# Attention scores in float32r: two heads on separate rows of the array instead of one wide product over both heads

## The chip, the cores and the metric

One core of a Trainium2 chip runs the whole program. The metric is the device time of one execution in microseconds (us); the kernel before takes 942.9 us, the median of three runs (940.86 to 945.25).

## The reference, cut to what matters

A linear-attention layer (batch B = 4, H = 8 heads, S = 768 positions, D = 48 channels per head) feeds two mixture-style layers of matrix products:

```python
for t in range(S):
    cur = np.einsum('bhd,bhe->bhde', u[None] * kt, vt)
    y[:, :, t] = np.einsum('bhd,bhde->bhe', rt, state + cur)
    state = w[None, :, :, None] * state + np.einsum('bhd,bhe->bhde', kt, vt)
...
x = y as [B*S, H*D]                       # 3072 x 384
m = ((x @ w_a) * (x @ w_b)) @ w_out       # d_ff 1536
out = (((m @ w1) * (m @ w2)) @ w3) @ w_out2   # d_ff 1024
```

All data are float32.

## The kernel before

**Tiling.** The positions are cut into 6 chunks of C = 128. A *unit* u is one chunk of one batch element: u = 4c + b, 24 units in all; "step c" is the four units of chunk c. The 8 heads lie in 4 pairs p; a pair has its first head in partitions 0 to 47 and its second in 64 to 111 (`XR`, line 179), 112 partitions in all. Inside a chunk the recurrence is written with matrices: per head a 128x128 matrix of scores k-times-r (functions `scores`, `scores_f`), masked and given its diagonal (`a_evac`, `a_diag`), then y = state times r plus scores times v (`y_mm`, lines 408 to 421), and the state is moved on by k times v (`s_mm`, `s_decay`, `s_upd`).

**Two ways to compute the scores.** Units 0 to 3 are done ahead (`scores_0`). Units 4 to 7 (u < `U_R` = 8) take `scores_f`, line 364: plain float32, for each pair p one 48x128 by 48x128 product per head, the two heads on rows 0 to 47 and rows 64 to 111 of the array, each head into its own PSUM tile (one tile for the first heads of all pairs, one for the second heads). From unit 8 on (step 2) the kernel splits k and r into a float32r high part and a float32r rest (`kth`, `ktl`; `rbh`, `rbl`) and adds three products, high-high, high-rest, rest-high (lines 381 to 383). There r lies in a tile of 256 columns per pair: columns 0 to 127 hold the first head in partitions 0 to 47, columns 128 to 255 the second head in partitions 64 to 111, and everything else is zero (memsets, lines 594 and 595). So one product over 112 rows with 128 columns of weights and 256 moving columns gives both heads; a PSUM tile holds two pairs, and `scores` is called in two halves, `scores(u, 0)` and `scores(u, 1)`.

**The order of heads.** Which half holds which head follows from this: with `scores_f` the halves of the score tile are "all first heads, all second heads" (0, 2, 4, 6, 1, 3, 5, 7), with the wide product they are 0, 1, 2, ... 7. `head(u, i)` on line 358 says so, and `y_mm` goes through the heads in that order: its product for head h writes rows 0 to 47 of the output for an even h and 64 to 111 for an odd one, that is, it uses one or the other half of the array's columns (48 columns of weights).

**What sets the order of the work.** The schedule is written by hand. `unit_slots` (line 508) cuts a unit into 8 slots; slots of the units of chunk q+1 are merged (`merge`, line 539) between the pieces of the first mixture layer on chunk q: `ab_mm` (line 631, products of 128x128 weights and 512 columns in float32r) and `m_mm` (line 676). Slot 0 has `scores(u, 0)` and the scaling of the next unit's r, slot 1 `scores(u, 1)` and `a_evac` of the first half, slot 2 the second half and `prep_hi` (the casts to float32r on ScalarE), slots 3 and 4 `prep_rl` (the rest of r, once per head of a pair, on GpSimd), slot 4 `y_mm` and `s_mm`, slot 5 the evacuation of y and `prep_kl`, slot 6 `s_upd`, which adds the new part to the state on VectorE. Scores, y and the state's products all take their PSUM tile from one pool of two buffers (`ps_at`, line 176, tile name `at`), in turn.

Of the kernel before, what the change touches and what calls it, by code (L numbers as in the profile page):

```python
# [7 lines left out]
F32 = mybir.dt.float32  # L8
F32R = mybir.dt.float32r
# [4 lines left out]
ALU = mybir.AluOpType  # L14
# [5 lines left out]
NP = H // 2  # L20
C = 128
# [30 lines left out]
U_R = 2 * B  # L52
# [102 lines left out]
def rwkv_moe_kernel(ctx, tc, rkT, nat, wu, wab, wout, w12, w3T, wo2, r_in, k_in, v_in, w_in, u_in, out):  # L155
    nc = tc.nc
    mm = nc.tensor.matmul
# [5 lines left out]
    def flat(ap):  # L163
        return ap.rearrange("p a b -> p (a b)")

    with tc.manual_schedule():
        const = tc.alloc_tile_pool(name="const", bufs=1, side="left")
        wabp = tc.alloc_tile_pool(name="wabp", bufs=1, side="left")
        att = tc.alloc_tile_pool(name="att", bufs=2, side="left")
# [6 lines left out]
        ps_at = tc.alloc_tile_pool(name="ps_at", bufs=2, space=PSUM)  # L176
        k_0 = xtp.tile([128, 2, B, DM], F32, tag="xt", name="k_0")[:, 0]

        XR = [(0, D), (64, 64 + D)]
# [5 lines left out]
        def load_rk(u):  # L185
            if u < NU:
                rk_t[u] = (wabp.tile([112, 2, NP * C], F32, tag=("w1h", "w1l", "w2h", "w2l")[u], name="rk")
                           if u < B else att.tile([112, 2, NP * C], F32, name="rk"))
                nc.sync.dma_start(out=rk_t[u], in_=rkT[u])
# [3 lines left out]
        def load_nat(u):  # L193
            if u < B:
                nc.sync.dma_start(out=v_0[:, u, :], in_=nat[u, :, 2, :])
            elif u < NU:
                nat_t[u] = att.tile([128, 3, DM], F32, name="natt")
                nc.sync.dma_start(out=nat_t[u], in_=nat[u])

        def v_of(u):  # L200
            return v_0[:, u, :] if u < B else nat_t[u][:, 2, :]
# [97 lines left out]
        for p in range(NP):  # L299
            nc.vector.tensor_tensor_scan(  # L300
                out=pos[:, p, 1:], data0=wc[:, p:p + 1].to_broadcast([112, HALF]), data1=zer,
# [5 lines left out]
        nc.vector.tensor_copy(out=tk, in_=tr[:, :, ::-1])  # L307
        wC = const.tile([112, NP, 1], F32, name="wC")
        nc.vector.tensor_tensor(out=wC, in0=pos[:, :, HALF:], in1=pos[:, :, HALF:], op=ALU.mult)
        rbh = att.tile([112, NP, 2 * C], F32R, name="rbh", bufs=1)  # L310
        rbl = att.tile([112, NP, 2 * C], F32R, name="rbl", bufs=1)
        s_t = [att.tile([112, NP, 112], F32, name=f"s{b}", bufs=1) for b in range(B)]

        rf_t, kth_t, ktl_t, d_t, a_t, kn_t, at_ps, xt = {}, {}, {}, {}, {}, {}, {}, {}

        kf_t, pr_t, y3_t = {}, {}, {}

# [7 lines left out]
            eng.tensor_tensor(out=kf_t[u], in0=kf_t[u], in1=flat(tk), op=ALU.mult)  # L325

        def prep_hi(u):
            for x, (a, e) in enumerate(XR):
                nc.scalar.copy(out=rbh[a:e, :, x * C:(x + 1) * C], in_=rf_t[u][a:e])  # L329
            kth_t[u] = att.tile([112, NP * C], F32R, name="kth", bufs=1)  # L330
            nc.scalar.copy(out=kth_t[u], in_=kf_t[u])

        def prep_rl(u, x, eng):
            a, e = XR[x]
            h, l = (t[a:e, :, x * C:(x + 1) * C] for t in (rbh, rbl))
            eng.tensor_tensor(out=l, in0=rf_t[u][a:e], in1=h, op=ALU.subtract)  # L336

        def prep_kl(u, eng):
            ktl_t[u] = att.tile([112, NP * C], F32R, name="ktl", bufs=1)
# [12 lines left out]
        def k_nat(u):  # L352
            if u < NU - B:
                k = k_0[:, u, :] if u < B else nat_t[u][:, 1, :]
                kn_t[u] = k if u < B else att.tile([128, DM], F32, name="kn", bufs=1)
                nc.gpsimd.tensor_tensor(out=kn_t[u], in0=k, in1=tnat.rearrange("p a x d -> p (a x d)"), op=ALU.mult)

        def head(u, i):

            return i if u >= U_R else i % 4 * 2 + i // 4  # L360

        def scores_f(ps, r, k):

            for p in range(NP):
                s = slice(p * C, (p + 1) * C)
                for x, (r0, r1) in enumerate(XR):
                    mm(ps[x][:, p, :], lhsT=k[r0:r1, s], rhs=r[r0:r1, s], start=True, stop=True)

        def scores(u, hf):
            if u < U_R:  # L370
                if hf == 0:
                    for x in range(2):
                        at_ps[u, x] = ps_at.tile([128, NP, C], F32, name="at")
                    scores_f([at_ps[u, x] for x in range(2)], flat(rf_t[u]), kf_t.pop(u))
                return
            ps = at_ps[u, hf] = ps_at.tile([128, 4, C], F32, name="at")
            for q in range(2):
                p = 2 * hf + q
                o = flat(ps[:, 2 * q:2 * q + 2, :])
                ks = slice(p * C, (p + 1) * C)  # L380
                mm(o, lhsT=kth_t[u][:, ks], rhs=rbh[:, p, :], start=True, stop=False)
                mm(o, lhsT=kth_t[u][:, ks], rhs=rbl[:, p, :], start=False, stop=False)
                mm(o, lhsT=ktl_t[u][:, ks], rhs=rbh[:, p, :], start=False, stop=True)

        def a_evac(u, hf):
            if hf == 0:
                a_t[u] = (wop.tile([128, H, C], F32, tag=("woh1", "wol1")[u % 2], name="a_0")
                          if u < B else att.tile([128, H, C], F32, name="a_sc", bufs=1))
            nc.vector.tensor_tensor(
                out=a_t[u][:, 4 * hf:4 * hf + 4, :], in0=at_ps.pop((u, hf)),  # L390
                in1=mask.rearrange("p (o n) -> p o n", o=1).to_broadcast([128, 4, C]), op=ALU.mult)

        def a_diag(u, hf):
            d = d_t[u][:, 4 * hf:4 * hf + 4] if u >= U_R else d_t[u].rearrange("p (q x) -> p x q", x=2)[:, hf, :]
            nc.vector.copy_predicated(  # L395
                out=a_t[u][:, 4 * hf:4 * hf + 4, :],
                mask=ident.bitcast(I32).rearrange("p (o n) -> p o n", o=1).to_broadcast([128, 4, C]),
                data=d.rearrange("p (h o) -> p h o", o=1).to_broadcast([128, 4, C]))
# [9 lines left out]
        def y_mm(u):  # L408
            c, b = divmod(u, B)
            ps = at_ps["y", u] = ps_at.tile([112, NP, C], F32, name="at")  # L410
            v, a = nat_t[u][:, 2, :], a_t.pop(u)

            for p in range(NP):
                mm(ps[:, p, :], lhsT=s_t[b][:, p, :], rhs=rf_t[u][:, p, :], start=(p == 0), stop=False,  # L414
                   skip_group_check=True)
            for i in range(H):
                h = head(u, i)
                r0, r1 = XR[h % 2]
                mm(ps[r0:r1, h // 2, :], lhsT=v[:, h * D:(h + 1) * D], rhs=a[:, i, :], start=False, stop=True,  # L419
                   skip_group_check=True)  # L420
            rf_t.pop(u)
# [45 lines left out]
        def s_mm(u):  # L467
            c, b = divmod(u, B)
            v = v_of(u)
            nat_t.pop(u, None)  # L470
            if c == NC - 1:
                return
            ps = (ps_at.tile([112, NP, D], F32, name="at") if c else
                  ps_m.tile([112, NP, D], F32, tag=("m2", "m0")[u % 2], name="s_ps"))
            at_ps["s", u] = ps
            kn = kn_t.pop(u)
            for p in range(NP):
                for x, (r0, r1) in enumerate(XR):
                    hs = slice((2 * p + x) * D, (2 * p + x + 1) * D)
                    mm(ps[r0:r1, p, :], lhsT=kn[:, hs], rhs=v[:, hs],  # L480
                       start=True, stop=True)

        def s_decay(u):
            c, b = divmod(u, B)
            if c < NC - 1:
                nc.gpsimd.tensor_tensor(out=s_t[b], in0=s_t[b], in1=wC.to_broadcast([112, NP, 112]), op=ALU.mult)
# [21 lines left out]
        def unit_slots(u):  # L508
            n = u + 1
            nxt = n < NU  # L510
            pool = nc.gpsimd

            def after(f, *a):
                if nxt:
                    f(n, *a)

            def after_r(f, *a):
                if nxt and n >= U_R:
                    f(n, *a)

            return [
                lambda: (scores(u, 0), after(prep_r, pool)),
                lambda: (scores(u, 1), a_evac(u, 0), after(prep_k, pool)),
                lambda: (a_evac(u, 1), a_diag(u, 0), after_r(prep_hi), k_nat(u)),
                lambda: (a_diag(u, 1), after_r(prep_rl, 0, pool)),

                lambda: (y_mm(u), s_mm(u), after_r(prep_rl, 1, pool)),
                lambda: (load_rk(u + 2), load_nat(u + 2), y_evac(u), (u + 1) % B == 0 and y_shuffle(u // B), s_decay(u),
                         after_r(prep_kl, pool), after(prep_d, 0)),
                lambda: (s_upd(u), after(prep_d, 1)),  # L530
                lambda: after(prep_d, 2),
            ]
# [58 lines left out]
        prep_0(1)  # L591
        both_a(0)
        diag_0(0)
        nc.gpsimd.memset(rbh.bitcast(F32), 0.0)
        nc.gpsimd.memset(rbl.bitcast(F32), 0.0)
        for t in s_t:
            nc.gpsimd.memset(t, 0.0)

# [516 lines left out]
```

## Time and profile before

| | |
|---|---|
| runs | 942.9 us median (940.86, 942.9, 945.25) |
| the profiled execution | 940.6 us, its span 938.9 us |
| TensorE matmul busy | 898.6 us (96%) |
| VectorE, ScalarE, GpSimd busy | 478.8, 344.0, 306.5 us |
| mean granted TensorE clock | 0.979 of full speed |

The span is what the trace covers, from the first to the last instruction; 1.7 us of the execution lie around it. Busy TensorE time is made of records that overlap: a 512-column product is recorded with 0.39 us although the next one starts 0.23 us later. What a stretch costs is read from the starts, not from the lengths. A float32 product leaves two records, a float32r product one. The scores in float32r run from 158.9 us (unit 8) to 490.9 us (unit 23).

### The profile page before, as it was taken

The numbers are of one execution on the slowest core, as the hardware profiler recorded it, in microseconds if no ns is written. First come the engines' busy times: TensorE is split into PE (matmuls) and PEld (weight loads), VectorE is DVE, ScalarE is ACT, GpSimd is POOL, SyncE is SP. The second block draws the span as 40 slices with busy tenths as digits, with TensorE's granted clock in tenths as the row PEclk, the third lists the DMA queues.
The fourth block names the chain that finished last, engine by engine and source line by source line (L and its number), as shares of the span: only waits on it lengthen the run. The fifth ranks groups of instructions, "written<-read, shape, count | busy, mean of one in ns | idle before, by whom it ended". The sixth has DMA issues, their size and how long they took to land.

```text
span 938.9 us, 12503 instructions
## 1 busy us (share of the span) xinstructions
PE 898.6 (96%) x4898; PEld 766.0 (82%) x4898; DVE 478.8 (51%) x684; ACT 344.0 (37%) x721; POOL 306.5 (33%) x245
## 2 busy tenths in 40 slices
PE   7778889999999999999999989899999999999997
PEld 7656678888888888888888867799988888888886
DVE  8799994545344544454442777765322222323222
ACT  4555653322322232223221775755422222222221
POOL 4566766555355626543420342322200000000000
PEclk9789889999999999999999999999999999999999
DMA  9534532212212211122102435443110010100001
GB/s 276 170 115 149 165 112 62 79 46 79 61 60 75 64 59 65 46 62 80 45 1 84 146 124 159 140 157 106 34 45 23 35 35 34 34 34 1 34 1 37
DMA packets 26065, 73.56 MB, mean 78 GB/s; under 512 B 3152, under 2 KB 7376, under 8 KB 26000
## 3 DMA queue, kind: packets, MB, share of 16 engines
q1 hardware_dynamic: 26000, 72.70, 24.6%
q8 instruction: 40, 0.66, 0.3%
q14 instruction: 25, 0.20, 0.1%
HBM read 61.28 MB, written 9.44 MB: 75 GB/s over the span
## 4 chain that ended last, share of the span: by engine, by line
PE 80%; DVE 11%; DMA 4%; issue 3%; ACT 1%; SPq 0%; DVEq 0%
PE ab L635 45%; PE m L686 4%; PE m L687 4%; PE m L688 4%; PE at L783 4%; DVE cvt L114 3%; PE o L807 3%; PE o L806 3%; PE o L808 3%; DVE cvt L117 2%; PE at L419 2%; PE at L414 2%; DVE cvt L98 1%; DMA stg_t<-in_wout_dram 1%; DVE gl L666 1%
## 5 line engine op out<-in xcount | busy, mean ns | idle before, releaser
L660 DVE TENSOR_TENSOR g<-g,ab 128x512 f32<-128x512 f32 x120 | 82.2, 685 | 269.1 <-PE ab L635 261.3
L635 PE MATMUL ab<-xt,w12h 128*128 128x512 f32 x576 | 177.5, 389 | 0.0
L661 ACT CAST gh<-g 128x512 fp32r<-128x512 f32 x120 | 74.5, 621 | 263.4 <-DVE g L660 263.4
L654 ACT COPY g<-ab 128x512 f32<-128x512 f32 x120 | 70.1, 584 | 247.4 <-PE ab L635 246.9
L666 DVE TENSOR_TENSOR gl<-g,gh 128x512 fp32r<-128x512 f32 x120 | 107.1, 893 | 65.0 <-ACT gh L661 65.0
L635 PEld LDWEIGHTS ab<-xt,w12h 128*128 128x128 f32 x576 | 107.5, 188 | 18.9
L635 PE MATMUL ab<-xt,w12l 128*128 128x512 f32 x288 | 112.0, 389 | 0.0
L687 PE MATMUL m<-gl,woh 128*128 128x512 f32 x216 | 86.4, 400 | 9.0 <-DVE gl L666 9.0
L686 PE MATMUL m<-gh,woh 128*128 128x512 f32 x216 | 87.3, 404 | 1.3 <-ACT gh L661 1.3
L336 POOL TENSOR_TENSOR rbl<-rk,rbh 48x512 fp32r<-48x512 f32 x32 | 49.3, 1542 | 120.1 <-ACT rbh L329 118.9
L688 PE MATMUL m<-gh,wol 128*128 128x512 f32 x216 | 85.2, 395 | 0.0
L635 PEld LDWEIGHTS ab<-xt,w12l 128*128 128x128 f32 x288 | 54.0, 188 | 11.2
L114 DVE SCALAR_TENSOR_TENSOR cvt<-stg_t,cvt 128x512 int32<-128x512 int32 x61 | 59.2, 970 | 0.3
L687 PEld LDWEIGHTS m<-gl,woh 128*128 128x128 f32 x216 | 41.3, 191 | 19.5 <-DVE gl L666 11.6
L117 DVE SCALAR_TENSOR_TENSOR cvt<-stg_t,cvt 128x512 int32<-128x512 int32 x61 | 54.5, 893 | 0.3
L686 PEld LDWEIGHTS m<-gh,woh 128*128 128x128 f32 x216 | 41.2, 191 | 12.4 <-ACT gh L661 3.3
L635 PE MATMUL ab<-xt,wab1h 128*128 128x512 f32 x144 | 47.0, 409 | 2.5 <-ACT wab1h L136 2.5
L688 PEld LDWEIGHTS m<-gh,wol 128*128 128x128 f32 x216 | 41.3, 191 | 8.7
L395 DVE COPY_PREDICATED a_sc<-ident,dg 128x512 f32<-128x512 int32 x40 | 46.3, 1197 | 0.0
L635 PE MATMUL ab<-xt,wab0h 128*128 128x512 f32 x144 | 45.3, 396 | 0.8 <-ACT g L654 0.8
L635 PE MATMUL ab<-xt,wab3h 128*128 128x512 f32 x144 | 45.9, 400 | 0.0
L635 PE MATMUL ab<-xt,wab2h 128*128 128x512 f32 x144 | 45.8, 400 | 0.0
(283 smaller groups left out, 1805.8 us busy)
## 6 DMA issues: line engine op xcount, KB each, us to landing
natt<-in_nat_dram SPq DMA_DIRECT2D x20, 576.0 KB, 5.0
rk<-in_rkT_dram SPq DMA_DIRECT2D x24, 448.0 KB, 4.2
stg_t<-in_wab_dram SPq DMA_DIRECT2D x18, 512.0 KB, 3.6
stg_t<-in_w3T_dram SPq DMA_DIRECT2D x16, 512.0 KB, 3.6
stg_t<-in_w_dram SPq DMA_DIRECT2D x12, 512.0 KB, 3.7
stg_t<-in_wout_dram SPq DMA_DIRECT2D x9, 512.0 KB, 3.5
m_d<-m_sb SPq DMA_DIRECT2D x18, 256.0 KB, 2.3
stg_t<-m_d SPq DMA_DIRECT2D x18, 256.0 KB, 2.6
```

The lines of the kernel that those rows point to most:

```text
L114: nc.vector.scalar_tensor_tensor(out=f, in0=w[:, :, 1], scalar=-0x40000000, in1=f, op0=ALU.bitwise_and, op1=ALU.bitwise_or)
L117: nc.vector.scalar_tensor_tensor(out=f, in0=w[:, :, 0], scalar=29, in1=f, op0=ALU.logical_shift_right, op1=ALU.bitwise_or)
L336: eng.tensor_tensor(out=l, in0=rf_t[u][a:e], in1=h, op=ALU.subtract)
L395: nc.vector.copy_predicated(out=a_t[u][:, 4 * hf:4 * hf + 4, :], mask=ident.bitcast(I32).rearrange("p (o n) -> p o n", o=1).to_broadcast([ ...
L635: mm(ps, lhsT=w[i][:, k, cs], rhs=x[:, j, k, :], start=(n == 0), stop=(n == 3 * KD - 1))
L654: nc.scalar.copy(out=t["g"], in_=t["a"])
L660: nc.vector.tensor_tensor(out=g, in0=g, in1=t["b"], op=ALU.mult)
L661: nc.scalar.copy(out=gh, in_=g)
L666: nc.vector.tensor_tensor(out=gl, in0=t["g"], in1=gh, op=ALU.subtract)
L686: mm(m_ps[q][k], lhsT=wh[:, j, cs], rhs=gh, start=(f == 0), stop=False)
L687: mm(m_ps[q][k], lhsT=wh[:, j, cs], rhs=gl, start=False, stop=False)
L688: mm(m_ps[q][k], lhsT=wl[:, j, cs], rhs=gh, start=False, stop=(f == NF1 - 1))
```

## The change

Units from 8 on now use the layout of `scores_f` for the three float32r products as well: the high part and the rest of r are plain 112 x 512 tiles (`rh`, `rl`), each product takes 48 rows, 128 columns of weights and 128 moving columns, and the two heads of a pair follow each other on rows 0 to 47 and rows 64 to 111, each into its own PSUM tile. All 24 products of a unit stand in slot 0, which takes both `at` buffers at once. `head` now gives the order 0, 2, 4, 6, 1, 3, 5, 7 for every unit, `a_diag` follows it, the cast of r is one instruction, the rest of r is one instruction (slot 3), and the two memsets are gone.

```diff
-        rbh = att.tile([112, NP, 2 * C], F32R, name="rbh", bufs=1)
-        rbl = att.tile([112, NP, 2 * C], F32R, name="rbl", bufs=1)
...
         def prep_hi(u):
-            for x, (a, e) in enumerate(XR):
-                nc.scalar.copy(out=rbh[a:e, :, x * C:(x + 1) * C], in_=rf_t[u][a:e])
+            rh_t[u] = att.tile([112, NP * C], F32R, name="rh", bufs=1)
+            nc.scalar.copy(out=rh_t[u], in_=flat(rf_t[u]))
...
-        def prep_rl(u, x, eng):
-            a, e = XR[x]
-            h, l = (t[a:e, :, x * C:(x + 1) * C] for t in (rbh, rbl))
-            eng.tensor_tensor(out=l, in0=rf_t[u][a:e], in1=h, op=ALU.subtract)
+        def prep_rl(u, eng):
+            rl_t[u] = att.tile([112, NP * C], F32R, name="rl", bufs=1)
+            eng.tensor_tensor(out=rl_t[u], in0=flat(rf_t[u]), in1=rh_t[u], op=ALU.subtract)
...
         def head(u, i):
-            return i if u >= U_R else i % 4 * 2 + i // 4
+            return i % 4 * 2 + i // 4
...
-        def scores(u, hf):
+        def scores(u):
+            ps = [ps_at.tile([128, NP, C], F32, name="at") for _ in XR]
+            for x in range(2):
+                at_ps[u, x] = ps[x]
             if u < U_R:
-                if hf == 0:
...
+                scores_f(ps, flat(rf_t[u]), kf_t.pop(u))
                 return
-            ps = at_ps[u, hf] = ps_at.tile([128, 4, C], F32, name="at")
-            for q in range(2):
-                p = 2 * hf + q
-                o = flat(ps[:, 2 * q:2 * q + 2, :])
-                ks = slice(p * C, (p + 1) * C)
-                mm(o, lhsT=kth_t[u][:, ks], rhs=rbh[:, p, :], start=True, stop=False)
-                mm(o, lhsT=kth_t[u][:, ks], rhs=rbl[:, p, :], start=False, stop=False)
-                mm(o, lhsT=ktl_t[u][:, ks], rhs=rbh[:, p, :], start=False, stop=True)
+            kh, kl, rh, rl = (t.pop(u) for t in (kth_t, ktl_t, rh_t, rl_t))
+            for p in range(NP):
+                s = slice(p * C, (p + 1) * C)
+                for n, (k, r) in enumerate(((kh, rh), (kh, rl), (kl, rh))):
+                    for x, (r0, r1) in enumerate(XR):
+                        mm(ps[x][:, p, :], lhsT=k[r0:r1, s], rhs=r[r0:r1, s], start=(n == 0), stop=(n == 2))
...
-                lambda: (scores(u, 0), after(prep_r, pool)),
-                lambda: (scores(u, 1), a_evac(u, 0), after(prep_k, pool)),
+                lambda: (scores(u), after(prep_r, pool)),
+                lambda: (a_evac(u, 0), after(prep_k, pool)),
                 lambda: (a_evac(u, 1), a_diag(u, 0), after_r(prep_hi), k_nat(u)),
-                lambda: (a_diag(u, 1), after_r(prep_rl, 0, pool)),
+                lambda: (a_diag(u, 1), after_r(prep_rl, pool)),
...
-        nc.gpsimd.memset(rbh.bitcast(F32), 0.0)
-        nc.gpsimd.memset(rbl.bitcast(F32), 0.0)
```

**TensorE at unit 8, the first unit with float32r scores.** `at` is the PSUM tile of the scores, `kth` and `ktl` are the weights, `rbh` and `rbl` (now `rh`, `rl`) what moves; `ab` is the first mixture layer. Before, the first half of the unit, three wide products for each of two pairs, then six products of `ab`:

```order
L635 MATMUL ab<-xt,wab0l 128x512
L381 MATMUL at<-rbh,kth 128x256
L382 MATMUL at<-rbl,kth 128x256
L383 MATMUL at<-rbh,ktl 128x256
L381 MATMUL at<-rbh,kth 128x256
L382 MATMUL at<-rbl,kth 128x256
L383 MATMUL at<-rbh,ktl 128x256
L635 MATMUL ab<-xt,wab0h 128x512 x2
L635 MATMUL ab<-xt,wab0l 128x512
```

With the change, at the same place, the whole unit, two heads in each row (x2):

```order
L378 MATMUL at<-rh,kth 128x128 x2
L378 MATMUL at<-rl,kth 128x128 x2
L378 MATMUL at<-rh,ktl 128x128 x2
L378 MATMUL at<-rh,kth 128x128 x2
L378 MATMUL at<-rl,kth 128x128 x2
L378 MATMUL at<-rh,ktl 128x128 x2
L378 MATMUL at<-rh,kth 128x128 x2
L378 MATMUL at<-rl,kth 128x128 x2
L378 MATMUL at<-rh,ktl 128x128 x2
L378 MATMUL at<-rh,kth 128x128 x2
L378 MATMUL at<-rl,kth 128x128 x2
L378 MATMUL at<-rh,ktl 128x128 x2
```

The second half has moved up by one slot, and 12 products of 256 columns have become 24 of 128. `y_mm` keeps its place and its count; only the heads inside it change places, which the names in this list do not tell.

**GpSimd in the slots of unit 7, where unit 8 is prepared.** `s_186` and `s_184` are the same tile, the state. Before:

```order
L137 TENSOR_TENSOR wab5l<-cvt,wab5h 128x512
L336 TENSOR_TENSOR rbl<-rk,rbh 48x4x128 x2
L486 TENSOR_TENSOR s_186<-s_186,wC 112x448
L340 TENSOR_TENSOR ktl<-rk,kth 112x512
L345 TENSOR_TENSOR pr<-natt,u_bc 128x384
```

With the change:

```order
L137 TENSOR_TENSOR wab5l<-cvt,wab5h 128x512
L333 TENSOR_TENSOR rl<-rk,rh 112x512
L481 TENSOR_TENSOR s_184<-s_184,wC 112x448
L337 TENSOR_TENSOR ktl<-rk,kth 112x512
L342 TENSOR_TENSOR pr<-natt,u_bc 128x384
```

Two instructions over 48 partitions have become one over 112; nothing else moves on this engine there.

## Rows read from the trace of the kernel before

**Rows 1.** The page's first part: busy time of each engine and its share of the span.

```profile
PE 898.6 (96%) x4898; PEld 766.0 (82%) x4898; DVE 478.8 (51%) x684; ACT 344.0 (37%) x721; POOL 306.5 (33%) x245
```

**Rows 2.** Busy time of each engine in the stretch of the float32r scores; the columns are the stretch, its length, then PE, PEld, DVE, ACT, POOL, the granted clock, the share of DMA and GB/s.

```profile
158.00:497.00 339.00, 339.00 (x1973) 284.84 (x1972) 162.15 (x223) 97.67 (x178) 158.54 (x126) 1.00 0.19 57
```

**Rows 3.** TensorE in order of time, the first half of unit 15's scores with the products around it: start, length to the end of the last of its records, instruction, count.

```profile
309.17 0.39 PE L635 MATMUL ab<-xt,wab4l 128*128 128x512 f32 x1
309.39 0.28 PE L381 MATMUL at<-rbh,kth 112*128 112x256 f32 x1
309.51 0.28 PE L382 MATMUL at<-rbl,kth 112*128 112x256 f32 x1
...
310.08 0.64 PE L635 MATMUL ab<-xt,wab4h 128*128 128x512 f32 x2
310.56 0.40 PE L635 MATMUL ab<-xt,wab4l 128*128 128x512 f32 x1
```

**Rows 4.** TensorE in order of time around unit 7's float32 scores, two heads on separate rows (16 records for 8 products).

```profile
131.78 0.40 PE L635 MATMUL ab<-xt,wab4l 128*128 128x512 f32 x1
132.11 1.16 PE L367 MATMUL at<-rk 48*128 48x128 f32 x16
133.20 0.50 PE L686 MATMUL m<-gh,woh 128*128 128x512 f32 x1
133.53 0.39 PE L687 MATMUL m<-gl,woh 128*128 128x512 f32 x1
133.76 0.39 PE L688 MATMUL m<-gh,wol 128*128 128x512 f32 x1
```

**Rows 5.** The weight loads (PEld) of the same place in order of time; those of L686 and L687 are of float32r weights.

```profile
132.10 0.97 PEld L367 LDWEIGHTS at<-rk 48*128 48x128 f32 x16 [0.36 <-issue]
133.20 0.19 PEld L686 LDWEIGHTS m<-gh,woh 128*128 128x128 f32 x1
133.30 0.19 PEld L687 LDWEIGHTS m<-gl,woh 128*128 128x128 f32 x1
```

**Rows 6.** TensorE in order of time, `y_mm` (L414, L419) and `s_mm` (L480) of unit 7, heads in the order 0, 2, 4, 6, 1, 3, 5, 7.

```profile
141.31 0.39 PE L688 MATMUL m<-gh,wol 128*128 128x512 f32 x1
141.53 1.04 PE L414 MATMUL at<-rk,s 112*112 112x128 f32 x8
142.50 1.23 PE L419 MATMUL at<-a_sc,natt 128*48 128x128 f32 x13
143.46 0.29 PE L480 MATMUL at<-natt,kn 128*48 128x48 f32 x2
...
143.78 0.27 PE L419 MATMUL at<-a_sc,natt 128*48 128x128 f32 x1
143.89 0.52 PE L480 MATMUL at<-natt,kn 128*48 128x48 f32 x12
144.34 0.74 PE L635 MATMUL ab<-xt,wab5h 128*128 128x512 f32 x2
144.92 0.39 PE L635 MATMUL ab<-xt,wab5l 128*128 128x512 f32 x1
```

**Rows 7.** The same of unit 8, heads in the order 0 to 7.

```profile
168.29 0.39 PE L635 MATMUL ab<-xt,wab0l 128*128 128x512 f32 x1
168.51 1.04 PE L414 MATMUL at<-rk,s 112*112 112x128 f32 x8
169.48 1.08 PE L419 MATMUL at<-a_sc,natt 128*48 128x128 f32 x16
170.39 0.53 PE L480 MATMUL at<-natt,kn 128*48 128x48 f32 x16
170.85 0.50 PE L686 MATMUL m<-gh,woh 128*128 128x512 f32 x1
171.19 0.39 PE L687 MATMUL m<-gl,woh 128*128 128x512 f32 x1
171.42 0.40 PE L688 MATMUL m<-gh,wol 128*128 128x512 f32 x1
```

**Rows 8.** By tile: the casts and subtractions that prepare r and k, with minimum, median and maximum duration in ns, and the memset of one of the two r tiles.

```profile
L329 ACT CAST rbh<-rk x32: 608/618/624, 138.5 to 471.9; 48x512 fp32r<-48x512 f32 x32
L336 POOL TENSOR_TENSOR rbl<-rk,rbh x32: 1288/1657/1783, 143.8 to 473.8; 48x512 fp32r<-48x512 f32 x32
L594 POOL MEMSET rbh<- x1: 947/947/947, 8.9 to 8.9; 112x1024 f32 x1
L331 ACT CAST kth<-rk x16: 620/621/622, 140.9 to 472.5; 112x512 fp32r<-112x512 f32 x16
L340 POOL TENSOR_TENSOR ktl<-rk,kth x16: 1281/1282/1653, 147.9 to 475.5; 112x512 fp32r<-112x512 f32 x16
```

**Rows 9.** GpSimd early, behind the memsets, and what it waited for before its copy.

```profile
13.93 0.31 POOL L566 COPY vz<-v 128x96 f32<-128x96 f32 x1 [0.36 <-PE at L431]
```

**Rows 10.** The state's update on VectorE before unit 14's scores, those scores' first product, and unit 5's float32 scores, which waited for such an update.

```profile
286.19 0.71 DVE L496 TENSOR_TENSOR s<-at,s 48x192 f32<-48x192 f32 x2
...
289.07 0.28 PE L381 MATMUL at<-rbh,kth 112*128 112x256 f32 x1
...
77.11 0.48 PE L367 MATMUL at<-rk 48*128 48x128 f32 x2
78.45 1.13 PE L367 MATMUL at<-rk 48*128 48x128 f32 x14 [0.85 <-DVE s L496]
```

More of the change, by code (lines that the diff above doesn't have):

```diff
@@ L309, in rwkv_moe_kernel @@
         nc.vector.tensor_tensor(out=wC, in0=pos[:, :, HALF:], in1=pos[:, :, HALF:], op=ALU.mult)
-        rbh = att.tile([112, NP, 2 * C], F32R, name="rbh", bufs=1)
-        rbl = att.tile([112, NP, 2 * C], F32R, name="rbl", bufs=1)
         s_t = [att.tile([112, NP, 112], F32, name=f"s{b}", bufs=1) for b in range(B)]
-        rf_t, kth_t, ktl_t, d_t, a_t, kn_t, at_ps, xt = {}, {}, {}, {}, {}, {}, {}, {}
+        rf_t, rh_t, rl_t, kth_t, ktl_t, d_t, a_t, kn_t, at_ps, xt = {}, {}, {}, {}, {}, {}, {}, {}, {}, {}
         kf_t, pr_t, y3_t = {}, {}, {}
@@ L367, in scores_f @@
                     mm(ps[x][:, p, :], lhsT=k[r0:r1, s], rhs=r[r0:r1, s], start=True, stop=True)
-        def scores(u, hf):
+        def scores(u):
+            ps = [ps_at.tile([128, NP, C], F32, name="at") for _ in XR]
+            for x in range(2):
+                at_ps[u, x] = ps[x]
             if u < U_R:
-                if hf == 0:
-                    for x in range(2):
-                        at_ps[u, x] = ps_at.tile([128, NP, C], F32, name="at")
-                    scores_f([at_ps[u, x] for x in range(2)], flat(rf_t[u]), kf_t.pop(u))
+                scores_f(ps, flat(rf_t[u]), kf_t.pop(u))
                 return
-            ps = at_ps[u, hf] = ps_at.tile([128, 4, C], F32, name="at")
-            for q in range(2):
-                p = 2 * hf + q
-                o = flat(ps[:, 2 * q:2 * q + 2, :])
-                ks = slice(p * C, (p + 1) * C)
-                mm(o, lhsT=kth_t[u][:, ks], rhs=rbh[:, p, :], start=True, stop=False)
-                mm(o, lhsT=kth_t[u][:, ks], rhs=rbl[:, p, :], start=False, stop=False)
-                mm(o, lhsT=ktl_t[u][:, ks], rhs=rbh[:, p, :], start=False, stop=True)
+            kh, kl, rh, rl = (t.pop(u) for t in (kth_t, ktl_t, rh_t, rl_t))
[4 more added lines that the diff above has]
+                        mm(ps[x][:, p, :], lhsT=k[r0:r1, s], rhs=r[r0:r1, s], start=(n == 0), stop=(n == 2))
         def a_evac(u, hf):
@@ L393, in a_diag @@
         def a_diag(u, hf):
-            d = d_t[u][:, 4 * hf:4 * hf + 4] if u >= U_R else d_t[u].rearrange("p (q x) -> p x q", x=2)[:, hf, :]
+            d = d_t[u].rearrange("p (q x) -> p x q", x=2)[:, hf, :]
             nc.vector.copy_predicated(
@@ L521, in unit_slots @@
             return [
-                lambda: (scores(u, 0), after(prep_r, pool)),
-                lambda: (scores(u, 1), a_evac(u, 0), after(prep_k, pool)),
+                lambda: (scores(u), after(prep_r, pool)),
+                lambda: (a_evac(u, 0), after(prep_k, pool)),
                 lambda: (a_evac(u, 1), a_diag(u, 0), after_r(prep_hi), k_nat(u)),
-                lambda: (a_diag(u, 1), after_r(prep_rl, 0, pool)),
-                lambda: (y_mm(u), s_mm(u), after_r(prep_rl, 1, pool)),
+                lambda: (a_diag(u, 1), after_r(prep_rl, pool)),
+                lambda: (y_mm(u), s_mm(u)),
                 lambda: (load_rk(u + 2), load_nat(u + 2), y_evac(u), (u + 1) % B == 0 and y_shuffle(u // B), s_decay(u),
```

## The prediction

> **What bounds the kernel now.** I read the busy shares first: TensorE 96%, no other engine above 51% [rows 1]. Then the stretches: from 158 to 497 us, where all float32r scores lie, TensorE is busy 339 of 339 us at a granted clock of 1.00, VectorE, ScalarE and GpSimd about half or less [rows 2]. So in this stretch every nanosecond that a unit adds to TensorE's stream ends up in the time, and what other engines gain or lose does not. Then TensorE's instructions in order of time, start against start, around three things that the change touches: the float32r scores [rows 3], the float32 scores on separate rows that units 4 to 7 already run [rows 4, 5], and `y_mm` in the one and the other order of heads [rows 6, 7].
>
> **What six wide products cost.** From the last product before them to the third after them is 309.17 to 310.56, 1.39 us [rows 3]. Three of these steps are 512-column products, 0.23 us each (133.53 to 133.76 in [rows 4]), so six wide products cost 1.39 - 0.69 = 0.70 us and a unit 1.40 us. That is 0.115 us each.
>
> **The new scores, part by part.** The nearest rows are unit 7's float32 scores: the same 48 rows, 128 weight columns and 128 moving columns, two heads side by side. From 131.78 to 133.53 are 1.75 us, less two full steps 1.29 us for 8 pairs of records [rows 4]. The weight loads tell the pace inside: 16 loads in 0.97 us, each recorded with 0.19, so the last pair starts 0.78 us after the first, 0.111 us per pair [rows 5]. Eight pairs are 0.89 us; the other 0.40 us is paid once for going from all rows to half rows and back (the first gap is 0.33 instead of 0.23, the step after the way back 133.20 to 133.53 again 0.33) [rows 4]. The wide products use 112 rows and pay nothing like it.
>
> Now the pace of a pair in float32r, which no row shows at 128 columns. Moving 128 columns at the pace of the wide product (0.115 us for 256) would take 0.058 us. But each product also loads 128 columns of weights, and a float32r load keeps the loader for 0.10 us before the next can begin, 133.20 to 133.30 [rows 5]. Under a 512- or 256-column product that is hidden; under 128 columns it is the longer of the two. Two loads on different rows run side by side (two per 0.111 us, [rows 5]), so a pair costs about one load, not two. I take 0.111 us, the pace at which such pairs of loads are seen to run; the bounds are 0.058 (loads cost nothing) and 0.222 (a float32 product's two records, or pairs that do not overlap). A unit then costs 0.40 + 12 x 0.111 = 1.73 us, 0.33 more than before; 16 units: **+5.3 us**.
>
> Two rules of the Trainium skill pull in different directions here. "TensorEngine Tiling (Array Packing)", section Theoretical Speedup, promises up to twice the speed where the contraction is 64 or less; by it the scores would halve, 16 x -0.70 = -11.2, and the sum with the heads below would be -3.6 instead of +12.9. "TensorE: Matmul & The Clock Gate", section LDWEIGHTS, speaks against the change: a load takes its columns divided by 1.2 in ns whatever its rows, 107 ns for 128, with which the trace's 0.10 agrees; by it the scores would come to +4.5.
>
> **The order of heads.** `head` changes `y_mm` for units 8 to 23 without touching a shape. In unit 8, even and odd heads alternate, the two halves of the array's columns work side by side, and from the last full product before to the third after are 168.29 to 171.42, 3.13 us [rows 7]. In unit 7 the four even heads come first; they share one half and run one behind the other, the odd heads start late, and the state's products squeeze in between (143.46). The same stretch is 141.31 to 144.92, 3.61 us [rows 6]. Same instructions, same count: 0.48 us. Twelve units have the state's products behind them. The last four have none; for them I compare the last start of L419, 1.28 us after its first in unit 7 [rows 6], with 0.91 less one pair, 0.81 us, in unit 8 [rows 7]: 0.47. Together 12 x 0.48 + 4 x 0.47 = **+7.6 us**. This price is seen, not guessed, and falls on the saturated engine.
>
> **What comes at nothing.** ScalarE casts r in one instruction instead of two of 0.62 us, GpSimd subtracts once (1.28 us, as `ktl`) instead of twice (1.66) [rows 8]; both engines are half idle there [rows 2] and nothing waits for them. The two memsets (0.95 us each, [rows 8]) leave GpSimd early, where it waits for TensorE right behind them anyway [rows 9]; that gives nothing.
>
> **PSUM.** Slot 0 now needs both `at` buffers, so the scores also wait for `s_upd` of the unit before, one slot earlier than now. In unit 14, the tightest, it ends at 286.90 and the scores start at 289.07: 2.17 us of cover [rows 10], of which the slower `y_mm` takes 0.48. No wait, then.
>
> **Sum.** 5.3 + 7.6 = +12.9 us on the profiled execution's 940.6: 953.5. That execution lies 2.3 us under the median of the runs, 942.9; against the median the forecast is **955.8 us**, 1.4% slower. A measurement of this kernel can tell about 0.5% from no change.
>
> **Rivals.**
> - *The narrow product is cheap.* Loads do not bind, a pair costs 0.058 us: 0.40 + 0.70 = 1.10 us, -0.30 x 16 = -4.8; with the heads' 7.6 it is +2.8, 945.7 us, not slower that can be told. It decides where a pair costs less than about 0.07 us. "TensorE: Matmul & The Clock Gate", section Back-to-back issue gap, gives 56 ns for 128 columns on their own, and would make it about 945. For it: the engine moves 256 columns in 0.115. Against it: the load [rows 5]. Without the 0.40 us as well it would be -11.2 + 7.6, 939.3, still within 0.5%. Chance 0.09.
> - *The narrow product is dear*, or the change does not do what it says: float32r at 128 columns runs as float32 does (two records each), or the two rows do not overlap. A pair costs 0.222: 0.40 + 2.66 - 1.40 = 1.66 us, 26.6 for 16 units, with the heads 34.2: 977.1 us. For it: no row shows float32r under 256 columns. Against it: the overlap is seen in float32 [rows 4, 5]. Chance 0.14.
> - *The buffers bind.* If `s_upd` comes over 2 us later, TensorE stands in front of slot 0 as in unit 5, where 77.11 to 78.45 lost some 1.2 us [rows 10]: in one unit of each step 5 us more, 960.6. Chance 0.04.
> - *The order of heads costs nothing* behind other neighbours, and the loads are cheap: 942.9 - 4.8 = 938.1 or less. [Rows 6, 7] leave it little: 0.03.
>
> **How the numbers follow.** The forecast has 0.70. Its own spread: 0.107 to 0.12 us per pair is +12 to +15, and the runs scatter 2 us around their median, so 952 to 960. With the cheap case and the buffers' case the range 944 to 962 holds about 0.82; left out are the dear case and a gain. Faster by over 0.5% 0.03; within 0.5% 0.09; slower 0.88.
>
> **What would show it.** Right: 24 records per unit in pairs a few ns apart, a pair every 0.11 us, gaps of about 0.33 us on the way in and out, a body of some 1.5 us; L414 and L480 around `y_mm` in every unit as in [rows 6], 3.6 us from before to the third after; no waits before the scores; all stages outside 158 to 510 us as long as before. Wrong in the scores: pairs at 0.06 or 0.22 us. Wrong as a whole: the stretch of units 8 to 23 not longer by about 13 us.

## The result and the profile after

The changed kernel takes **951.7 us** (median of 6 runs, 950.26 to 953.12) against 942.8 before (6 runs): ratio 1.0103, 95% interval 1.0086 to 1.0120. Run a second time beside other kernels it gave 952.7 against 940.7, ratio 1.0123 (1.0106 to 1.0141). So it is slower by 1.0 to 1.2%, 9 to 12 us; the forecast was 12.9. Of the two profiled executions the spans differ by 951.1 - 938.9 = 12.2 us.

The page's first lines and the stretch of the float32r scores, which answer to [rows 1, 2]:

```profile
span 951.1 us, 12830 instructions
PE 912.7 (96%) x5090; PEld 775.3 (82%) x5090; DVE 469.6 (49%) x684; ACT 332.4 (35%) x705; POOL 274.7 (29%) x227
...
158.00:510.00 352.00, 352.00 (x2180) 292.41 (x2180) 151.88 (x225) 87.03 (x164) 131.63 (x111) 1.00 0.18 55
```

GpSimd lost 32 us of work and ScalarE 12, and none of that can be seen in the time: TensorE has no gap in the stretch, its clock stays at 1.00 (2.4 GHz), and it simply has more to do.

TensorE in order of time around unit 15's scores, answering to [rows 3, 4] (L378 is the new product, L628 the `ab` product, L414 now the product of scores and v):

```profile
313.80 0.39 PE L628 MATMUL ab<-xt,wab4l 128*128 128x512 f32 x1
314.12 0.33 PE L378 MATMUL at<-rh,kth 48*128 48x128 f32 x2
314.28 0.28 PE L378 MATMUL at<-rl,kth 48*128 48x128 f32 x2
...
315.40 0.28 PE L378 MATMUL at<-rh,ktl 48*128 48x128 f32 x2
315.60 0.74 PE L628 MATMUL ab<-xt,wab4h 128*128 128x512 f32 x2
316.18 0.39 PE L628 MATMUL ab<-xt,wab4l 128*128 128x512 f32 x1
```

Each row is a pair, two heads nearly at once, and the rows stand 0.11 us apart: from 314.28 to 315.40 are ten steps, 0.112 each. From 313.80 to the third product after, 316.18, are 2.38 us, less three steps of 0.23 leaves 1.69 us for a unit's scores; before it was 1.40. All 16 units have 1.68 to 1.69. The weight loads of the same place (PEld) keep the same step:

```profile
314.22 0.19 PEld L378 LDWEIGHTS at<-rl,kth 48*128 48x128 f32 x2
314.33 0.19 PEld L378 LDWEIGHTS at<-rh,ktl 48*128 48x128 f32 x2
```

And unit 8's `y_mm` and `s_mm` (L409, L414, L475), which answer to [rows 7] and look like [rows 6]:

```profile
167.81 0.39 PE L628 MATMUL ab<-xt,wab0l 128*128 128x512 f32 x1
168.03 1.04 PE L409 MATMUL at<-rk,s 112*112 112x128 f32 x8
169.00 1.23 PE L414 MATMUL at<-a_sc,natt 128*48 128x128 f32 x13
169.96 0.29 PE L475 MATMUL at<-natt,kn 128*48 128x48 f32 x2
...
170.39 0.52 PE L475 MATMUL at<-natt,kn 128*48 128x48 f32 x12
170.84 0.50 PE L679 MATMUL m<-gh,woh 128*128 128x512 f32 x1
171.18 0.39 PE L680 MATMUL m<-gl,woh 128*128 128x512 f32 x1
171.41 0.40 PE L681 MATMUL m<-gh,wol 128*128 128x512 f32 x1
```

From 167.81 to 171.41 are 3.60 us; before, in the same unit, 3.13. The state's products begin (169.96) before the last heads are through. So the two terms can be read off the trace: 16 x (1.69 - 1.40) = 4.6 us from the scores, 16 x 0.47 to 0.48 = 7.6 us from the order of heads, 12.2 together, which is the difference of the two spans (how far that agreement is chance, the last experiment shows).

### The profile page after: what moved, and what is told of

It reads as the page before. It is cut to its first block, busy times and chain, and to the rows that moved or that the text cites. A ratio compares the mean times of both kernels' runs of the same rounds, so it can differ in the third digit from the quotient of the medians.

```text
span 951.1 us, 12830 instructions
## 1 busy us (share of the span) xinstructions
PE 912.7 (96%) x5090; PEld 775.3 (82%) x5090; DVE 469.6 (49%) x684; ACT 332.4 (35%) x705; POOL 274.7 (29%) x227
## 4 chain that ended last, share of the span: by engine, by line
PE 80%; DVE 11%; DMA 4%; issue 3%; ACT 1%; SPq 0%; DVEq 0%
PE ab L628 45%; PE m L679 4%; PE m L680 4%; PE m L681 4%; PE at L776 4%; DVE cvt L114 3%; PE at L414 3%; PE o L800 3%; PE o L799 3%; PE o L801 3%; DVE cvt L117 3%; PE at L378 3%; PE at L409 2%; DVE cvt L98 1%; DMA stg_t<-in_wab_dram 1%
## 5 line engine op out<-in xcount | busy, mean ns | idle before, releaser
L628 PE MATMUL ab<-xt,w12h 128*128 128x512 f32 x576 | 178.0, 390 | 0.0
L659 DVE TENSOR_TENSOR gl<-g,gh 128x512 fp32r<-128x512 f32 x120 | 104.6, 872 | 65.7 <-ACT gh L654 65.7
L628 PEld LDWEIGHTS ab<-xt,w12h 128*128 128x128 f32 x576 | 108.0, 188 | 19.0
L628 PE MATMUL ab<-xt,w12l 128*128 128x512 f32 x288 | 112.3, 390 | 0.0
L628 PEld LDWEIGHTS ab<-xt,w12l 128*128 128x128 f32 x288 | 54.2, 188 | 11.3
L333 POOL TENSOR_TENSOR rl<-rk,rh 112x512 fp32r<-112x512 f32 x16 | 21.3, 1329 | 132.6 <-ACT rh L327 115.6
L114 DVE SCALAR_TENSOR_TENSOR cvt<-stg_t,cvt 128x512 int32<-128x512 int32 x61 | 59.2, 970 | 0.3
L117 DVE SCALAR_TENSOR_TENSOR cvt<-stg_t,cvt 128x512 int32<-128x512 int32 x61 | 56.6, 929 | 0.3
L679 PEld LDWEIGHTS m<-gh,woh 128*128 128x128 f32 x216 | 41.5, 192 | 12.9 <-ACT gh L654 3.2
L628 PE MATMUL ab<-xt,wab1h 128*128 128x512 f32 x144 | 47.3, 411 | 2.5 <-ACT wab1h L136 2.5
L628 PE MATMUL ab<-xt,wab0h 128*128 128x512 f32 x144 | 45.7, 399 | 0.8 <-ACT g L647 0.8
L628 PE MATMUL ab<-xt,wab2h 128*128 128x512 f32 x144 | 45.9, 400 | 0.0
L628 PE MATMUL ab<-xt,wab3h 128*128 128x512 f32 x144 | 45.3, 396 | 0.0
L628 PE MATMUL ab<-xt,wab4h 128*128 128x512 f32 x144 | 45.3, 396 | 0.0
```

What stands on the lines that cost most here:

```text
L114: nc.vector.scalar_tensor_tensor(out=f, in0=w[:, :, 1], scalar=-0x40000000, in1=f, op0=ALU.bitwise_and, op1=ALU.bitwise_or)
L117: nc.vector.scalar_tensor_tensor(out=f, in0=w[:, :, 0], scalar=29, in1=f, op0=ALU.logical_shift_right, op1=ALU.bitwise_or)
L628: mm(ps, lhsT=w[i][:, k, cs], rhs=x[:, j, k, :], start=(n == 0), stop=(n == 3 * KD - 1))
L659: nc.vector.tensor_tensor(out=gl, in0=t["g"], in1=gh, op=ALU.subtract)
L679: mm(m_ps[q][k], lhsT=wh[:, j, cs], rhs=gh, start=(f == 0), stop=False)
```

## Experiments

My theory has three parts, each with its price: the order of heads (0.47 to 0.48 us per unit), the load of 128 weight columns as the pace of a narrow pair (0.111 us), and the way to half rows and back (0.35 to 0.40 us per visit). The main rivals: the loss comes with the narrow scores alone; the columns and not the loads set the pace; the visit has no price of its own.

**The order alone, taken back.** The change with `y_mm` going through the heads alternately from unit 8 on:

```diff
-            for i in range(H):
+            for j in range(H):
+                i = j % 2 * 4 + j // 2 if u >= U_R else j
```

> The change with one thing more: from unit 8 on y_mm takes the heads alternately again (0, 1, 2, ... 7), the scores stay as changed. Theory (the order of heads costs 0.47 to 0.48 us per unit): the stretch around y_mm falls from 3.61 to 3.13 us in 16 units, 7.6 us in all, so 951.7 - 7.6 = 944.1 us, within 0.5% of before. Rival (the whole loss lies in the scores, the order is hidden or depends on what follows): y_mm shrinks but what stands behind it starts no earlier, 951.7 us.

945.4 us, ratio 1.0039 (1.0023 to 1.0056), +2 to +5 us on before instead of +9 to +12: by ratios 6 to 8 us came back. Unit 8 in the trace:

```profile
167.34 0.39 PE L629 MATMUL ab<-xt,wab0l 128*128 128x512 f32 x1
...
168.53 1.08 PE L415 MATMUL at<-a_sc,natt 128*48 128x128 f32 x16
169.44 0.53 PE L476 MATMUL at<-natt,kn 128*48 128x48 f32 x16
...
170.47 0.40 PE L682 MATMUL m<-gh,wol 128*128 128x512 f32 x1
```

All 16 records of the heads stand together again, and 167.34 to 170.47 is 3.13 us, the value of before. What is left against before, 4.6 us by the scores' rows, lies inside the interval. The rival falls.

**The order alone, put into the kernel before.** Wide scores, zeros and slots as they were:

```diff
-            for i in range(H):
+            for j in range(H):
+                i = j % 4 * 2 + j // 4 if u >= U_R else j
```

> The kernel before with one thing changed: from unit 8 on y_mm takes the even heads first, then the odd ones; wide scores, zeros and slots as before. Theory: 16 x 0.475 = 7.6 us more, 942.8 + 7.6 = 950.4 us, the larger part of the change's loss from one line. Rival (the price comes with the narrow scores): 942.8 us.

949.7 us, ratio 1.0083 (1.0063 to 1.0102), 5.9 to 9.6 us more; expected 7.6. Unit 8 again:

```profile
167.74 0.39 PE L636 MATMUL ab<-xt,wab0l 128*128 128x512 f32 x1
...
168.93 1.23 PE L420 MATMUL at<-a_sc,natt 128*48 128x128 f32 x13
169.89 0.29 PE L481 MATMUL at<-natt,kn 128*48 128x48 f32 x2
...
171.34 0.40 PE L689 MATMUL m<-gh,wol 128*128 128x512 f32 x1
```

3.60 us. One line of the change, which moves no instruction from its place, is worth more than the whole rebuilding of the scores.

**Twice the loads, the same columns.** The change with each product cut in two of 64 moving columns:

```diff
+                for z in range(2):
+                    zs = slice(z * HALF, (z + 1) * HALF)
+                    sz = slice(p * C + z * HALF, p * C + (z + 1) * HALF)
...
-                        mm(ps[x][:, p, :], lhsT=k[r0:r1, s], rhs=r[r0:r1, s], start=(n == 0), stop=(n == 2))
+                            mm(ps[x][:, p, zs], lhsT=k[r0:r1, s], rhs=r[r0:r1, sz], start=(n == 0), stop=(n == 2))
```

> The change with each narrow product cut into two of 64 moving columns: same columns moved, twice the weight loads. Theory (a pair costs one load of 128 columns, 0.111 us, however few columns move): 24 pairs per unit instead of 12, 16 x 12 x 0.111 = 21.3 us more, 973 us. Rival (a float32r product of under 256 columns moves at half pace, two cycles a column, and the load is hidden): a pair takes 0.056 us, 951.7 us.

991.5 us, ratio 1.053 (1.049 to 1.057): more than either theory said. The pace of a pair is as the load theory has it. Unit 12, first and last pairs:

```profile
261.78 0.39 PE L631 MATMUL ab<-xt,wab0l 128*128 128x512 f32 x1
262.10 0.30 PE L381 MATMUL at<-rh,kth 48*128 48x64 f32 x2
262.23 0.28 PE L381 MATMUL at<-rl,kth 48*128 48x64 f32 x2
...
264.69 0.28 PE L381 MATMUL at<-rh,ktl 48*128 48x64 f32 x2
...
265.47 0.39 PE L631 MATMUL ab<-xt,wab0l 128*128 128x512 f32 x1
```

262.23 to 264.69 are 22 steps of 0.112 us, with half the columns in each; 261.78 to 265.47 less three steps is 3.00 us, 1.31 more than the change, 21 us for 16 units. The rest, some 18 us, is behind other units' scores. Unit 11, whose scores run from 229.93 to 232.7 (columns as in [rows 2], then TensorE in order of time):

```profile
229.90:232.70 2.80, 2.80 (x49) 2.77 (x48) 0.00 (x0) 0.59 (x1) 0.00 (x0) 0.99 0.00 0
232.70:235.00 2.30, 2.30 (x7) 1.82 (x7) 0.69 (x1) 0.00 (x0) 0.00 (x0) 0.50 0.00 0
```

```profile
232.77 1.22 PE L631 MATMUL ab<-xt,wab4h 128*128 128x512 f32 x2
233.79 0.63 PE L631 MATMUL ab<-xt,wab4l 128*128 128x512 f32 x1
234.21 1.05 PE L631 MATMUL ab<-xt,wab4h 128*128 128x512 f32 x2
...
236.21 0.39 PE L631 MATMUL ab<-xt,wab4l 128*128 128x512 f32 x1
236.44 0.40 PE L682 MATMUL m<-gh,woh 128*128 128x512 f32 x1
```

After 2.8 us of short products, recorded as busy throughout, the granted clock falls to 0.50 (1.2 GHz) and full products take 0.42 us instead of 0.23 until about 236: nine of them from 232.77 to 236.44, 3.67 us, where 0.58 + 7 x 0.23 = 2.2 would do. That happens behind 13 of the 16 units, not behind units 12, 16 and 20; why not there is open. The theory of the load stands, and a second cost that no theory named is seen beside it. In the change itself the scores last half as long and the clock stays at 1.00.

**Twice the columns, the same loads.** Each product moves 256 columns, those of two pairs, against the weights of one; the kernel leaves out the right scores, and only its time is of use:

```diff
+                q = min(p, NP - 2)
+                s2 = slice(q * C, (q + 2) * C)
...
-                        mm(ps[x][:, p, :], lhsT=k[r0:r1, s], rhs=r[r0:r1, s], start=(n == 0), stop=(n == 2))
+                        mm(flat(ps[x][:, q:q + 2, :]), lhsT=k[r0:r1, s], rhs=r[r0:r1, s2], start=(n == 0), stop=(n == 2))
```

> The change with each product moving 256 columns, those of two pairs, against the weights of one (the additional columns are overwritten or wrong scores; only the time is of use). Same number of loads, twice the columns. Theory (the load sets the pace): a pair of products costs 0.115 us instead of 0.111, 952 to 952.5 us: the additional columns are free. Rival (columns set the pace, two cycles each): 0.222 us a pair, 16 x 12 x 0.111 = 21.3 us more, 973 us.

954.3 us, ratio 1.0135 (1.0111 to 1.0159). Unit 15:

```profile
314.36 0.28 PE L380 MATMUL at<-rl,kth 48*128 48x256 f32 x2
314.48 0.28 PE L380 MATMUL at<-rh,ktl 48*128 48x256 f32 x2
...
315.54 0.28 PE L380 MATMUL at<-rh,ktl 48*128 48x256 f32 x2
```

Ten steps in 1.18 us: 0.118 a pair for twice the columns, a twentieth more. With half, the same and twice the columns the pair takes 0.112, 0.112 and 0.118 us: up to 256 columns something that a pair pays whatever it moves sets the pace, and the columns ride along. The rival (two cycles a column) falls on both sides. That the fixed part is the load and not, say, the issue of two loads and two products, is read from rows: the load records keep the step of 0.11 us, and the state's products in [rows 7], with 48 weight columns and 48 moving columns, put 16 records, eight pairs with their loads, between 170.39 and 170.85, under 0.06 us a pair. No run changed the number of weight columns alone.

**Two visits instead of one.** The change with pairs 0 and 1 in slot 0 and pairs 2 and 3 in slot 1:

```diff
-                lambda: (scores(u), after(prep_r, pool)),
-                lambda: (a_evac(u, 0), after(prep_k, pool)),
+                lambda: (scores(u, 0), after(prep_r, pool)),
+                lambda: (scores(u, 1), a_evac(u, 0), after(prep_k, pool)),
```

> The change with the narrow scores in two places again: pairs 0 and 1 in slot 0, pairs 2 and 3 in slot 1, same 24 products. Theory (going to half rows and back costs about 0.35 us each time, beside 12 x 0.112 us for the pairs): a unit's scores rise from 1.69 to 2.04 us, 16 x 0.35 = 5.6 us more than the change. Rival (the 0.35 us is no price of a visit, the pairs are simply slower than 0.112): no difference from the change.

958.8 us, ratio 1.0192 (1.0172 to 1.0213); the change beside it 1.0123. The difference of 0.0069 is 6.5 us, with each ratio known to some 2 us either way. Unit 8, first visit:

```profile
158.31 0.39 PE L636 MATMUL ab<-xt,wab0l 128*128 128x512 f32 x1
158.63 0.33 PE L386 MATMUL at<-rh,kth 48*128 48x128 f32 x2
158.79 0.28 PE L386 MATMUL at<-rl,kth 48*128 48x128 f32 x2
...
159.44 0.73 PE L636 MATMUL ab<-xt,wab0h 128*128 128x512 f32 x2
160.01 0.39 PE L636 MATMUL ab<-xt,wab0l 128*128 128x512 f32 x1
```

158.31 to 160.01 less three steps is 1.01 us for six pairs; six at 0.112 are 0.67, so 0.34 is the visit, paid again for the second: in this trace each of the 32 visits takes 1.01 to 1.03 us, 0.34 more per unit than the change, 5.5 us for 16 units. The visit has its own price.

**A version without float32r scores.** All units as units 4 to 7, plain float32, and the heads alternately in every unit:

```diff
-U_R = 2 * B
+U_R = NU
...
-            for i in range(H):
+            for j in range(H):
+                i = j % 2 * 4 + j // 2
```

> All units take the float32 scores of units 4 to 7 (no casts, no rests), and y_mm takes the heads alternately in every unit. Theory: scores 1.29 us per unit against 1.40 of the kernel before, 16 x -0.10 = -1.6 us; y_mm 0.48 us less in units 4 and 7, up to as much in 5 and 6, -1.0 to -1.9: together -2.6 to -3.5 us, 939.3 us where before is 942.5, ratio 0.996 to 0.997. Rival (the casts on ScalarE and GpSimd cost something too): faster than that.

937.3 us, ratio 0.9964 (0.9950 to 0.9977): faster than both kernels, than the one before by 2 to 5 us; expected were 2.6 to 3.5. The scores cost what was expected, 158.01 to 160.00 less three steps, 1.30 us; unit 8, and the scores of unit 23 (485.47):

```profile
158.01 0.39 PE L629 MATMUL ab<-xt,wab0l 128*128 128x512 f32 x1
158.32 1.16 PE L364 MATMUL at<-rk 48*128 48x128 f32 x16
...
160.00 0.39 PE L629 MATMUL ab<-xt,wab0l 128*128 128x512 f32 x1
...
485.47 1.16 PE L364 MATMUL at<-rk 48*128 48x128 f32 x16
```

The part on units 4 and 7 was wrong. Unit 7:

```profile
141.70 0.42 PE L415 MATMUL at<-a_sc,natt 128*48 128x128 f32 x2
142.35 0.96 PE L415 MATMUL at<-a_sc,natt 128*48 128x128 f32 x13 [0.23 <-DVE a_sc L390]
```

Taken alternately the odd heads come second, and there VectorE has not finished their half of the scores: the gain turns into a wait. In the old order the four even heads cover that half's work and no such wait is seen [rows 6]. From unit 8's scores to unit 23's are 327.15 us, before 328.67 (158.87 to 487.54, shown under the last experiment): 0.10 us less a unit, which is the scores' own gain. So the casts and rests that fell away gave nothing there, and of the gain only the 1.6 us of the scores' term are shown. Where the rest came from is open, and that the whole still fell into the expected range is in part luck.

**The change once more,** beside the last two:

> The changed kernel itself beside the others of this job. Its stretch of units 8 to 23 is 12.2 us longer in the profile, the ratio of its runs says 9.7 us (8.1 to 11.3). If that difference is scatter of the stretches before and behind, the ratio comes out nearer 1.013; if the change gives 2 to 3 us back elsewhere, it stays near 1.010.

Ratio 1.0123 (1.0106 to 1.0141), 11.6 us where the first series gave 9.7. The first product of the scores of unit 8 and of unit 23, in the kernel before and then in this run:

```profile
158.87 0.28 PE L381 MATMUL at<-rbh,kth 112*128 112x256 f32 x1
487.54 0.28 PE L381 MATMUL at<-rbh,kth 112*128 112x256 f32 x1
...
159.43 0.33 PE L378 MATMUL at<-rh,kth 48*128 48x128 f32 x2
499.66 0.33 PE L378 MATMUL at<-rh,kth 48*128 48x128 f32 x2
```

Between the two lie 328.67 us before and 340.23 us in this run; in the first trace of the change it is 340.23 us as well (158.19 to 498.42). That is 0.77 us for each of 15 units, as the two terms say, and 12.3 us for 16. So the price inside the stretch is the same in both traces. What scatters is the time in front of it (unit 8's scores start at 158.87 us before, at 158.19 and 159.43 in the two traces of the change) and behind it; that the two spans differ by the very sum of the terms, 12.2 us, is in part luck. The first series' interval, 8.1 to 11.3 us, leaves the 12.3 out, the second's, 10.0 to 13.3, holds them; that the change gives a microsecond back elsewhere is not excluded.

## Why the prediction was right

It was right in sign, size and mechanism: +9 to +12 us measured, 12.9 forecast, and the terms separate as forecast.

- *What bounds.* Right: TensorE is busy throughout units 8 to 23, before [rows 2] and after, and 43 us less work on ScalarE and GpSimd over the program brought nothing that can be seen.
- *The order of heads, +7.6.* Right to a tenth: 3.60 and 3.13 us in both directions (taken out of the change, put into the kernel before). This term rested on rows of the kernel before that show both orders side by side, and that is why it was exact.
- *The scores, +5.3.* Measured 4.6. The pace of a pair, the one price no row showed, came out at 0.112 us as taken. That the float32 rows had the same 0.111 [rows 5] is in part luck: they cannot tell the load from the columns. In [rows 7] the 16 float32 records of L419, also with 128 moving columns but with only 48 weight columns, run from 169.48 to 170.39, 0.11 us for two heads as well. What bore the reading was the 0.10 us of the float32r load, and what showed it is the run with 64 columns. The mis-sized term is the visit to half rows: forecast 0.40, measured 0.34 to 0.35. From the first narrow product to the next full one, twelve float32r pairs take 1.48 us (314.12 to 315.60) and eight float32 pairs 1.09 (132.11 to 133.20, [rows 4]): 0.39 us for four pairs that by their pace should take 0.45. The float32 rows from which the visit was priced carry some 0.06 us that float32r does not pay.
- *The two rules of the Trainium skill.* The promise of up to twice the speed for contractions of 64 or less ("TensorEngine Tiling (Array Packing)", section Theoretical Speedup) is not borne out here: the pairs do overlap, but the scores went from 1.40 to 1.69 us. The rule on the length of a load ("TensorE: Matmul & The Clock Gate", section LDWEIGHTS), 107 ns for 128 columns, agrees with 0.112 per pair at 64, 128 and, nearly, 256 columns.
- *PSUM.* Right: no wait. In unit 14 the state's update ends at 290.78 and the scores start at 292.99, still 2.2 us. The 0.48 us that the forecast took off this cover did not go, since the slower `y_mm` stands in front of the update and of the scores alike:

```profile
290.07 0.71 DVE L491 TENSOR_TENSOR s<-at,s 48x192 f32<-48x192 f32 x2
...
292.99 0.33 PE L378 MATMUL at<-rh,kth 48*128 48x128 f32 x2
```

- *The rivals.* The cheap product and the dear product are both excluded by the pairs' steps in the trace; the buffers did not bind; the order was not free.
- *The level.* Here the forecast was 4 us high. It put the difference on the median of the runs, 942.9, because the profiled execution of before, 940.6, lay under it. That execution lies below all six timed runs of the kernel before, and the profiled one of the change, 953.1, is the highest of its six, whose median is 951.7. The difference of the spans is met within 0.7 us. Of the times of the runs, the first series (8.1 to 11.3 us) leaves the forecast's 12.9 out, the second (10.0 to 13.3) holds it; the mis-sized visit explains 0.7 of the shortfall, and for the rest the cause is not shown beyond the scatter outside the stretch.

## What to carry to other kernels

A product on part of the rows still pays a whole weight load: in float32r here, 128 weight columns set a floor of 0.11 us under each step, so cutting a 256-column product into narrower ones saves nothing that TensorE can use, and changing between whole and half rows costs about 0.35 us each time. Look at the order in which products alternate between halves of the array's columns: it changes no instruction's shape and no count, and here it was the larger half of the loss. And when a change bundles such things, price them one by one from a place of the old trace that already does it the new way.

## What was not expected

With 64 moving columns per product the granted clock dropped to 0.50 behind the scores, although the records before it say busy in 2.80 of 2.80 us; the 1.5 us lost there, behind 13 of the 16 units, cost nearly as much again as the additional loads (18 beside 21 us). With 128 columns and half the time, in the change itself, the clock stayed at 1.00.
